# Query ratio on GpSimd, kv products from PSUM column 8, and half of wv issued from ScalarE's queue

## The chip, the cores and the metric

The kernel runs on one core of one Trainium2 chip. The metric is device microseconds of one execution. The kernel before takes 271.44 us (median of 3 runs, 271.33 to 271.71).

## The reference

The input x is 2048 tokens of 640 bf16 numbers. It goes through a layer norm, and then through a linear attention with a learned feature map and through a gated MLP, and the two results are added to x.

```python
xn = layernorm(x)
# A: 32 heads of 20 columns
q, k, v = split(xn @ wqkv)
pq, pk = q @ w_phi, k @ w_phi                      # per head, 20 x 20
phi_q = concat(softmax(pq), softmax(-pq))          # 40 features
phi_k = concat(softmax(pk), softmax(-pk))
kv = phi_k^T @ v ;  z = sum_s phi_k                # per head: 40 x 20 and 40
o = (phi_q @ kv) / (phi_q @ z + 1e-6)
# B
h = silu(xn @ w1) * (xn @ w3)                      # 1536 columns
out = x + o @ wo + h @ w2
```

## The kernel before

**Tiling.** Tokens are cut into 16 tiles `t` of 128 (partitions). The 640 columns are 5 chunks of 128 (`DC`), the 1536 hidden columns 12 chunks (`FC`), and the MLP works on 4 blocks of 512 tokens (`NB`). xn is kept transposed (`xnT`), so that token tiles serve as weights of TensorE and blocks of 512 tokens as moving data. For the kv sums and the query products the 32 heads are taken three at a time, in 11 groups (`NG`, the last has two heads); a head has 20 columns and one for the denominator, so a group has 63 columns, the last 42.

**Stages.** (1) `first_loads` issues the loads: token tile 0 in two halves (one from SyncE's queue, one from ScalarE's), tiles 1 and 2, the two halves of `wv` (the v columns of wqkv), tile 3, the first third of w1 and w3, and so on. Warm-up matmuls on a tile of zeros run meanwhile (`idle`). Tile 0 is normalised on VectorE; the sums of tile 1 are made on ScalarE (`act_sum`). The first four tiles are transposed on TensorE, each followed by its v product in ten matmuls (`v_part`: five with the first half of `wv`, five with the second). (2) `fold_mm` multiplies w_phi into the k and q weights (`Wkp`, `Wqp`). (3) `k_tile` makes the key features, `k_norm` normalises them: VectorE sums (`S`) and takes reciprocals (`rS`), and GpSimd multiplies the features `ekt` with them, two operations for each token tile. (4) `kv_sum` makes kv of all tiles in four parts of four tiles, `kv_store` masks and stores it as `KVc`. (5) For each tile, `q_proj` makes the query features `eq` (ScalarE exponentials), `q_norms` scales them, a transposing DMA makes `eqT`, `q_tok` multiplies them with `KVc` and divides by the denominator, and another transposing DMA makes `oT`. (6) `mlp(b, fc)` is one chunk of the hidden columns of one block: ten matmuls of 512 columns into a pair of PSUM banks, a tanh on ScalarE (`th`), and two VectorE operations (`t1`, in the profile `t`, then `hT`), the first of which reads the first bank of the pair. (7) `out_tile` adds the two output products and x.

**The query scaling.** The two softmaxes differ by a factor for each head only, and one of the two sums cancels against the denominator. So `q_ratio(t)` makes the two sums of a head (`Sq`) by a VectorE reduction, takes the reciprocal of the second on VectorE (`rq`) and multiplies it with the first; `q_scale(t)` then multiplies half of the features with the ratio on GpSimd. Where GpSimd is expected to be free, it adds the two halves of the features before the reduction (`q_half`, tile `half`).

**Order.** No order is written out by hand. Fourteen streams (generators, lines 732 to 916) offer their next step; a planner estimates with costs for each operation when each step could start, takes the earliest, and so lays down one order for each engine. Engines then run their lists in order, with semaphore waits where data or PSUM banks pass from one engine to another. A change of a cost or of an engine can therefore move other steps too. PSUM's 8 banks of 512 f32 columns are used in four pairs; `held` keeps the pair in which kv is summed. The MLP is the stream that fills the time in which TensorE would wait for others.

The operations of the profile are all recorded at line 102 (DMA issues at line 114), so they are told apart by the names of tiles and not by lines.

Of the kernel before, what the change touches and what calls it, by code (L numbers as in the profile page):

```python
# [3 lines left out]
ACT = mybir.ActivationFunctionType  # L4
ALU = mybir.AluOpType
# [4 lines left out]
D = 640  # L10
H = 32
# [6 lines left out]
NG = 11  # L18
# [231 lines left out]
def bass_parallel_sum__linear_kernel_hedgehog__glu_gated_swiglu__prompt_kernel(  # L250
# [16 lines left out]
    P = _Program(nc)  # L267
# [12 lines left out]
    def new(name, shape, dtype, offset=None):  # L280
        size = mybir.dt.size(dtype)
        for n in shape[1:]:
            size *= n
        return P.sbuf(name, shape, dtype, region(size) if offset is None else offset)
# [28 lines left out]
    wv = new("wv", [128, DC, D], bf, RKV + 6400)  # L313
# [10 lines left out]
    eqT = [new(f"eqT{i}", [128, NG, 128], bf, (RKV, RE + 27648)[i // 2] + 5632 + 2816 * (i % 2)) for i in range(4)]  # L324
# [8 lines left out]
    KVc = new("KVc", [128, H * 21], bf, RW)  # L333
# [6 lines left out]
    PS = nc.alloc_psum_tensor("PS", [128, 8 * 512], f32)  # L340
# [3 lines left out]
    def bank(k, cols=512, off=0, rows=128):  # L344
        return PS[0:rows, k * 512 + off:k * 512 + off + cols]
# [5 lines left out]
    def mm(o, l, r, start, stop, shared=False, cost=None):  # L351
        n = free(r)
        P.op("PE", "matmul", [o], [l, r], (o, l, r),
             dict(start=start, stop=stop, skip_group_check=shared),
             cost=max(n / 2400 + 0.003, 0.055) if cost is None else cost)
# [5 lines left out]
    def free(ap):  # L361
        n = 1
        for s in ap.shape[1:]:
            n *= s
        return n
# [5 lines left out]
    def tt(eng, o, a, b, f, fast=1):  # L371
        c = 0.16 + free(o) / 960 / fast if eng == "DVE" else 0.2 + free(o) * 1.7 / 1000
        P.op(eng, "tensor_tensor", [o], [a, b], (o, a, b, f), cost=c)

    def stt(o, a, s, b, f0, f1):
        P.op("DVE", "scalar_tensor_tensor", [o], [a, b], (),
             dict(out=o, in0=a, scalar=s, in1=b, op0=f0, op1=f1), cost=0.16 + free(o) / 960)
# [24 lines left out]
    wqkv_t = A_wqkv.rearrange("(c p) n -> p c n", p=128)  # L402
# [4 lines left out]
    def w13(a, b):  # L407
        P.dma("SP", w1_s[:, :, a:b], w1_t[:, :, a:b])
        P.dma("SP", w3_s[:, :, a:b], w3_t[:, :, a:b])

    def load_x(a, b):
        P.dma("SP", x_tok[:, a:b, :], x_t[:, a:b, :])

    def first_loads():
        def half_wv(a):
            P.dma("SP", wv[:, :, a:a + 320], wqkv_t[:, :, 2 * D + a:2 * D + a + 320])

        P.dma("SP", x_tok[:, 0, 0:320], x_t[:, 0, 0:320])
        P.dma("ACT", x_tok[:, 0, 320:D], x_t[:, 0, 320:D])
        load_x(1, 2)  # L420
        load_x(2, 3)
        half_wv(0)
        half_wv(320)
        load_x(3, 4)
        w13(0, 512)
        P.dma("SP", phi_s[:], phi_t)
        P.dma("SP", wqkT[:, DC:2 * DC, :], A_wqkv[:, D:2 * D], True)
        load_x(4, 8)
        load_x(8, 12)
        load_x(12, 16)  # L430
        P.dma("SP", wqkT[:, 0:DC, :], A_wqkv[:, 0:D], True)
# [152 lines left out]
    def group(g):  # L584
        return 3 * g, min(3, H - 3 * g)
# [46 lines left out]
    def q_sums(t):  # L632
        s = Sq[:, t % 4, :]
        i = eq[t % 4][:].rearrange("p (g c) -> p g c", c=128)[:, :, 0:120].rearrange("p g (n f) -> p g n f", f=DH)
        h = half[:, t % 2, :].rearrange("p (g n f) -> p g n f", n=6, f=10)
        return s[:, 0:66].rearrange("p (g n) -> p g n", n=6), i, h
# [5 lines left out]
    def q_ratio(t, halved):  # L642
        o, i, h = q_sums(t)
        i = h if halved else i
        P.op("DVE", "tensor_reduce", [o], [i], (o, i, AX.X, ALU.add), cost=0.12 + free(i) / 960)
        s = Sq[:, t % 4, :]
        r = rq[:, t % 3, :]
        sv = s[:, 0:64].rearrange("p (h s) -> p h s", s=2)
        P.op("DVE", "reciprocal", [r], [sv[:, :, 1]], (r, sv[:, :, 1]), cost=0.36)
        tt("DVE", r, r, sv[:, :, 0], ALU.mult)  # L650

    def q_scale(t):
        r = rq[:, t % 3, :]
# [10 lines left out]
    def q_tok(t, k):  # L664
        for g in range(NG):
            h, nh = group(g)
            c = 21 * h
            for a, b in ((c, min(c + 21 * nh, 512)), (max(c, 512), c + 21 * nh)):
                if a < b:
                    mm(bank(k, b - a, a), eqT[t % 4][:, g, :], KVc[:, a:b], a in (0, 512), b in (512, 21 * H), True,  # L670
                       max(0.026, (b - a) / 2400 + 0.003))
        p = PS[:, k * 512:k * 512 + 21 * H].rearrange("p (h c) -> p h c", c=21)
        den = den_s[:, t % 2, :]
        sv = Sq[:, t % 4, 0:64].rearrange("p (h s) -> p h s", s=2)
        stt(den, sv[:, :, 0], DEN_EPS, p[:, :, DH], ALU.mult, ALU.add)
        P.op("DVE", "reciprocal", [den], [den], (den, den), cost=0.36)
        tt("DVE", o_tok[:, t % 3, :].rearrange("p (h c) -> p h c", c=DH), p[:, :, 0:DH],
           den.unsqueeze(2).to_broadcast([128, H, DH]), ALU.mult)
# [52 lines left out]

    def norms():
        yield lambda: (first_loads(), consts())
        yield lambda: act_sum(1, ACT.Copy, bst[:, 1, 0:1])
        yield lambda: (ln_half(0, 0), ln_half(0, 1), ln_rstd(0, 1))
# [135 lines left out]
    def q_norms():  # L871
        for t in range(T):
            while done["qp"] <= t:
                yield None
            halved = P.free["POOL"] < P.free["PE"] + 2.0
            if halved:
                yield lambda t=t: q_half(t)
            yield lambda t=t, halved=halved: q_ratio(t, halved)
            yield lambda t=t: q_scale(t)
            done["qn"] = t + 1  # L880
# [8 lines left out]
    def q_toks():  # L889
        for t in range(T):  # L890
            while done["qd"] <= t or not done["kv"]:
                yield None
            yield lambda t=t: q_tok(t, banks(2))
            done["q"] = t + 1
# [129 lines left out]
```

## Time and profile before

| | |
|---|---|
| median of 3 runs | 271.44 us (271.33 to 271.71) |
| the profiled execution | 271.57 us |
| its span, first instruction to last | 269.8 us, 4835 instructions |
| busy: TensorE, VectorE, ScalarE, GpSimd | 263.6, 177.9, 99.6, 97.5 us |
| granted TensorE clock | 1.0 throughout |
| DMA | 27.73 MB, mean 103 GB/s |

In the rows, PE is TensorE (PEld its weight loads), DVE VectorE, ACT ScalarE, POOL GpSimd, SP SyncE; a q behind the name stands for the engine's queue of issues. Times are microseconds from the start of the span. A row of the timeline has start, duration, engine, line, operation, output<-inputs, shapes and count; in brackets stands the idle time of that engine ahead of it and what ended it. Some matmul records are missing (1958 matmuls are shown beside 1978 weight loads): a group of ten may be shown as nine.

### The profile page before, as it was taken

The page shows a single profiled execution, that of the slowest core. Times are in us where ns is not written, and L with a number is a line of the kernel's source. Part 1 is how long each engine was busy: PE and PEld are TensorE (multiplying, and loading weights), DVE is VectorE, ACT ScalarE, POOL GpSimd, SP SyncE. Part 2 cuts the span into 40 slices and gives each one's busy share as a digit, 9 for nine tenths or more (in the row PEclk, how much of TensorE's full clock was granted, in tenths as well). Part 3 has the DMA queues.
Part 4 walks back from the last instruction along what each step waited for, and adds up shares of the span by engine and source line. Part 5 has one row for each costly group of instructions (what it writes and reads, how often), then busy time and mean ns, then how long its engine had stood idle before and what let it go on. Part 6 is the DMA issues. An engine that isn't in the chain of part 4 may idle for free.

```text
span 269.8 us, 4835 instructions
## 1 busy us (share of the span) xinstructions
PE 263.6 (98%) x1958; PEld 161.9 (60%) x1978; DVE 177.9 (66%) x308; ACT 99.6 (37%) x193; POOL 97.5 (36%) x126
## 2 busy tenths in 40 slices
PE   7999999999989999999999999999999999999996
PEld 4656677776736555555555455544577777777774
DVE  4549899998899898888988878878712121212112
ACT  5547979988323434435242434242100000000000
POOL 4225848999993443644444434222000000000000
PEclk9999999999999999999999999999999999999999
DMA  6998695900093255455444460424211313131301
GB/s 193 282 309 179 147 220 116 308 10 2 4 327 72 49 102 80 80 99 102 87 80 89 91 80 10 93 57 78 49 51 52 97 49 97 51 97 49 93 31 49
DMA packets 63510, 27.73 MB, mean 103 GB/s; under 512 B 49792, under 2 KB 63488, under 8 KB 63488
## 3 DMA queue, kind: packets, MB, share of 16 engines
q1 hardware_dynamic: 63344, 27.35, 43.1%
q8 instruction: 15, 0.25, 0.4%
q10 hardware_dynamic: 144, 0.08, 0.1%
q14 instruction: 7, 0.06, 0.1%
HBM read 12.81 MB, written 2.62 MB: 57 GB/s over the span
## 4 chain that ended last, share of the span: by engine, by line
PE 74%; POOL 12%; DVE 9%; issue 3%; DMA 1%; DVEq 0%
PE PS L102 74%; POOL ekt L102 10%; DVE bst L102 4%; DVE x_tok L102 1%; POOL rstd L102 1%; DVE S L102 1%; DMA x_tok<-in_A_x_dram 1%; POOL v L102 1%; DVE hT L102 1%; DVE t L102 1%; DVE Sq L102 1%; DVE mv L102 0%; DVE rS L102 0%; POOL M L102 0%; DVE xres L102 0%
## 5 line engine op out<-in xcount | busy, mean ns | idle before, releaser
L102 PE MATMUL PS<-xnT,w_s 128*128 128x512 bf16 x463 | 105.8, 379 | 1.9 <-DVE t L102 0.8
L102 PEld LDWEIGHTS PS<-xnT,w_s 128*128 128x128 bf16 x480 | 45.5, 98 | 52.2 <-DVE t L102 1.3
L102 PE MATMUL PS<-w_s,hT 128*128 128x320 bf16 (+2 forms) x384 | 54.9, 299 | 0.0
L102 DVE TENSOR_TENSOR xres<-PS,xres 128x640 bf16<-128x640 f32 (+2 forms) x17 | 13.3, 785 | 60.0 <-PE PS L102 60.0
L102 ACT ACTIVATE th<-PS 128x512 f32<-128x512 f32 x48 | 28.8, 600 | 52.4 <-PE PS L102 52.4
L102 PEld LDWEIGHTS PS<-w_s,hT 128*128 128x128 bf16 x384 | 37.6, 98 | 14.6
L102 DVE SCALAR_TENSOR_TENSOR t<-th,PS 128x512 bf16<-128x512 f32 x48 | 32.7, 681 | 15.0 <-ACT th L102 14.6
L102 POOL TENSOR_TENSOR eq<-eq,rq 128x600 bf16<-128x600 bf16 (+1 forms) x32 | 22.6, 727 | 53.8 <-DVE rq L102 53.7
L102 POOL TENSOR_TENSOR ekt<-ekt,rS 128x640 bf16<-128x640 bf16 x32 | 39.5, 1265 | 0.6 <-DVE rS L102 0.6
L102 ACT ACTIVATE eq<-PS 128x600 bf16<-128x600 f32 (+1 forms) x72 | 24.6, 411 | 27.8 <-PE PS L102 27.6
L102 DVE SCALAR_TENSOR_TENSOR hT<-t,PS 128x512 bf16<-128x512 bf16 x48 | 33.0, 687 | 1.8 <-DVE t L102 0.2
L102 PE MATMUL PS<-wv,xnT 128*128 128x320 bf16 x160 | 24.8, 299 | 0.1
L102 PE MATMUL PS<-wo_s,oT 128*128 128x320 bf16 (+2 forms) x160 | 24.5, 299 | 0.0
L102 PE MATMUL PS<-Wkp,xnT 128*128 128x320 bf16 x160 | 23.9, 299 | 0.0
L102 ACT ACTIVATE ekt<-PS 128x640 bf16<-128x640 f32 x32 | 22.3, 703 | 3.8 <-PE PS L102 3.3
L102 PE MATMUL PS<-Wqp,xnT 128*128 128x128 bf16 (+1 forms) x157 | 23.3, 297 | 0.2
L102 DVE TENSOR_REDUCE S<-ekt 128x64 f32<-128x1280 bf16 x16 | 23.0, 1438 | 0.0
L102 POOL TENSOR_TENSOR half<-eq 128x660 f32<-128x660 bf16 x14 | 19.0, 1356 | 8.6 <-ACT eq L102 8.6
L102 PEld LDWEIGHTS PS<-wo_s,oT 128*128 128x128 bf16 x160 | 15.7, 98 | 6.3
L102 PEld LDWEIGHTS PS<-Wqp,xnT 128*128 128x128 bf16 x160 | 12.9, 98 | 10.7
L102 PEld LDWEIGHTS PS<-wv,xnT 128*128 128x128 bf16 x160 | 15.2, 98 | 6.8 <-DVE xnT L102 0.4
L102 PEld LDWEIGHTS PS<-Wkp,xnT 128*128 128x128 bf16 x160 | 15.5, 98 | 6.0
(55 smaller groups left out, 176.9 us busy)
## 6 DMA issues: line engine op xcount, KB each, us to landing
w_s<-in_B_w_dram SPq DMA_DIRECT2D x6, 640.0 KB, 6.2
xres<-in_A_x_dram SPq DMA_DIRECT2D x16, 160.0 KB, 2.3
out_dram<-xres SPq DMA_DIRECT2D x15, 160.0 KB, 1.8
x_tok<-in_A_x_dram SPq DMA_DIRECT2D x3, 640.0 KB, 6.3
w_s<-in_B_w_dram SPq DMA_DIRECT2D x1, 1920.0 KB, 8.0
wv<-in_A_wqkv_dram SPq DMA_DIRECT2D x2, 400.0 KB, 5.4
wo_s<-in_A_wo_dram SPq DMA_DIRECT2D x1, 800.0 KB, 8.4
x_tok<-in_A_x_dram SPq DMA_DIRECT2D x3, 160.0 KB, 3.3
```

The costliest lines, as they stand in the source:

```text
L102: o = _Op(eng, lambda: m(*args, **kw), r, w, cost)
```

## The change

It has three parts.

1. In `first_loads` the first half of `wv` is issued from ScalarE's queue, directly behind ScalarE's half of token tile 0, where it was issued from SyncE's queue behind token tile 2. What follows it on SyncE's queue (the second half of `wv`, tile 3, w1, w3 and all later loads) is issued one place earlier.
2. In `q_ratio` the product of the reciprocal with the first sum is made on GpSimd, where it was on VectorE.
3. In `q_tok` the products lie in PSUM from column 8 of the pair of banks, where they began at column 0. Eight groups of 63 columns are 504, so the border between the banks at column 512 falls between the eighth and the ninth group. Before, it cut the ninth group, which was done in two matmuls of 8 and 55 columns with the same weights. The planner's costs of these matmuls change with it.

```diff
     def first_loads():
-        def half_wv(a):
-            P.dma("SP", wv[:, :, a:a + 320], wqkv_t[:, :, 2 * D + a:2 * D + a + 320])
+        def half_wv(eng, a):
+            P.dma(eng, wv[:, :, a:a + 320], wqkv_t[:, :, 2 * D + a:2 * D + a + 320])
 
         P.dma("SP", x_tok[:, 0, 0:320], x_t[:, 0, 0:320])
         P.dma("ACT", x_tok[:, 0, 320:D], x_t[:, 0, 320:D])
         load_x(1, 2)
         load_x(2, 3)
-        half_wv(0)
-        half_wv(320)
+        half_wv("ACT", 0)
+        half_wv("SP", 320)
         load_x(3, 4)
...
         P.op("DVE", "reciprocal", [r], [sv[:, :, 1]], (r, sv[:, :, 1]), cost=0.36)
-        tt("DVE", r, r, sv[:, :, 0], ALU.mult)
+        tt("POOL", r, r, sv[:, :, 0], ALU.mult)
...
     def q_tok(t, k):
         for g in range(NG):
             h, nh = group(g)
-            c = 21 * h
-            for a, b in ((c, min(c + 21 * nh, 512)), (max(c, 512), c + 21 * nh)):
-                if a < b:
-                    mm(bank(k, b - a, a), eqT[t % 4][:, g, :], KVc[:, a:b], a in (0, 512), b in (512, 21 * H), True,
-                       max(0.026, (b - a) / 2400 + 0.003))
-        p = PS[:, k * 512:k * 512 + 21 * H].rearrange("p (h c) -> p h c", c=21)
+            a, b = 21 * h, 21 * (h + nh)
+            mm(bank(k, b - a, 8 + a), eqT[t % 4][:, g, :], KVc[:, a:b], g in (0, 8), g in (7, NG - 1), True, 0.031)
+        p = PS[:, k * 512 + 8:k * 512 + 8 + 21 * H].rearrange("p (h c) -> p h c", c=21)
```

With the change the planner lays down another order from the query stage on. TensorE's order is the same up to `q_proj(2)`; then an MLP chunk comes ahead of `q_proj(3)` and not behind it, two chunks and not one stand between the products of query tiles 0 and 1, and three and not two follow the last query tile's. On VectorE the reduction of query tile 1 moves behind `kv_store` and is made from GpSimd's `half`, as for the later tiles. On SyncE's queue some transposes `oT` and `eqT` change places.

## The prediction

> **What bounds the kernel now.** The page first: it says which engine fills the span.
>
> ```profile
> span 269.8 us, 4835 instructions
> PE 263.6 (98%) x1958; PEld 161.9 (60%) x1978; DVE 177.9 (66%) x308; ACT 99.6 (37%) x193; POOL 97.5 (36%) x126
> ```
>
> TensorE is busy for 263.6 of 269.8 us. So time can go in two ways only: TensorE gets less to do, or one of its few waits goes. The other engines matter where they make it wait. Next I read the waits of TensorE. The longest one in the middle of the kernel is "PE PS <- DVE t"; the timeline around it shows where it is from.
>
> ```profile
> 62.85 17.22 POOL L102 TENSOR_TENSOR ekt<-ekt,rS 128x640 bf16<-128x640 bf16 x14
> 69.22 4.24 PE L102 MATMUL PS<-v,ekt 128*128 128x63 bf16 x132
> 70.82 0.63 DVE L102 SCALAR_TENSOR_TENSOR t<-th,PS 128x512 bf16<-128x512 f32 x1
> 73.51 6.42 PE L102 MATMUL PS<-xnT,w_s 128*128 128x512 bf16 x29
> 74.57 0.60 ACT L102 ACTIVATE th<-PS 128x512 f32<-128x512 f32 x1 [4.90 <-PE PS L102]
> 75.96 4.16 DVE L102 TENSOR_TENSOR rq<-rq,Sq 128x32 f32<-128x32 f32 x1
> 80.04 0.68 DVE L102 SCALAR_TENSOR_TENSOR t<-th,PS 128x512 bf16<-128x512 f32 x1
> 80.20 1.41 POOL L102 TENSOR_TENSOR eq<-eq,rq 128x600 bf16<-128x600 bf16 x2
> 80.78 2.33 PE L102 MATMUL PS<-xnT,w_s 128*128 128x512 bf16 x10 [0.84 <-DVE t L102]
> 81.64 1.27 SPq L114 DMA_TRANSPOSE eqT<-eq  x1
> 82.94 1.52 PE L102 MATMUL PS<-v,ekt 128*128 128x63 bf16 x44
> ...
> L102 DVE TENSOR_TENSOR rq<-rq,Sq x16: 191/192/4160, 76.0 to 181.9; 128x32 f32<-128x32 f32 x16
> ...
>   DVE rq L102: 53.7, 15
> ```
>
> At 75.96 VectorE begins the product of the ratio of query tile 0. The tile view (min/median/max in ns) says that this operation takes 192 ns, but this one takes 4160: it ends when GpSimd's run of back-to-back key multiplications ends (62.85 + 17.22 = 80.07). Behind it in VectorE's queue stands the first operation on the MLP chunk whose tanh was ready at 75.17. It frees a bank that the fourth chunk needs, so it is late (80.04), and TensorE stops. The thirty matmuls from 73.51 go at 0.216 each (ten from 80.78 to 82.94), so they are issued by 79.99 and the wait is 80.78 - 79.99 = 0.79 us (the row's 0.84 is against the end of the last matmul shown; one record is missing).
>
> The Trainium skill ("SBUF — State Buffer", section "SBUF: two separate sides") says that a VectorE operation with two SBUF inputs and a GpSimd operation that reads SBUF exclude each other for a whole instruction. By that rule alone the wait here would be one GpSimd instruction at most, an estimate of 1.2 us (17.22 / 14), and TensorE would not notice; the row shows 3.97 us beyond the usual 0.19, so here the measured length decides.
>
> **The change, part by part. The ratio on GpSimd.** The operation leaves VectorE. There the tanh's reader, which also runs while GpSimd multiplies (70.82: 0.63 us, no delay), follows the reciprocal at about 75.96 and frees the bank at 76.6, and the fourth MLP chunk needs it at 79.99. The wait of 0.79 us goes; 3.3 us of slack stand in its place. What is late next there is kv's last part: it needs the last key tile (80.07) and is reached at 79.99 + 2.16 = 82.15, so it doesn't wait either. **Term 1: -0.79 us.**
>
> The operation costs GpSimd something that no row shows. The nearest row is a product of 40 columns with the ratio, the farthest plausible one VectorE's own 0.19:
>
> ```profile
> L102 POOL TENSOR_TENSOR eq<-eq,rq 128x40 bf16<-128x40 bf16 x16 | 4.0, 252 | 0.0
> ...
> DMA to landing us min/median/max: 3.5/3.6/5.3
> ...
> 89.18 0.52 PE L102 MATMUL PS<-KVc,eqT 128*128 128x63 bf16 x12
> 89.54 2.32 PE L102 MATMUL PS<-xnT,w_s 128*128 128x512 bf16 x9
> ```
>
> I take 0.25. The sixteen are 4 us, and half of tile 1's features adds one more operation; GpSimd waited 53.7 us for the ratio (the row "DVE rq", above), so the room is there. The wait itself is not new: GpSimd waited for VectorE's product at this place and now waits for VectorE's reciprocal. Behind it in GpSimd's queue stand the scaling and the next tile's `half`; behind the scaling come SyncE's transpose to `eqT` and TensorE's product. For tile 0 the scaling starts 0.25 later (80.45), the transpose is issued at 81.9, and lands 3.6 later (the median of `eqT`) at 85.5. TensorE reaches this product later: kv ends at 82.15 + 44 x 0.031 = 83.5, then ten query-projection steps, ten MLP matmuls and ten more projection steps (1.36 + 2.16 + 1.36) bring it to 88.4. Slack 2.9 us, so I cost it at nothing. If it were uncovered it would cost at most the 0.06 to 0.1 us by which 0.25 exceeds 0.19 plus a hand-over, for each tile: 1.6 us for sixteen.
>
> **The products from column 8.** A tile's products are 11 matmuls and not 12. The 12 take 0.36 us (89.18 to 89.54). For 11, ten of 63 and one of 42 columns, the kv sums are the row: 132 matmuls from 69.22 in 4.24 us, of which the last one's pass is about 0.18, so (4.24 - 0.18) / 131 = 0.031 each and 0.341 for 11. That saves 0.019 a tile. Bounds: nothing, if the pace is set by columns, which stay 672; and a full matmul of 0.031, 0.49 us for sixteen. I take the measured difference, 16 x 0.019. All lie on TensorE's path. **Term 2: -0.30 us.** The VectorE readers keep their shapes.
>
> **Half of wv from ScalarE's queue.** Here are the rows of the first 10 us, and one further on for the pace; below them stand the landing times of wv and three stretches of the windows view (length; busy us and count of PE, PEld, DVE, ACT, POOL; granted clock; DMA share; GB/s).
>
> ```profile
> 0.79 1.35 SPq L114 DMA_DIRECT2D x_tok<-in_A_x_dram  x3
> 0.79 0.39 ACTq L114 DMA_DIRECT2D x_tok<-in_A_x_dram  x1
> 1.21 1.28 ACT L102 ACT_TABLE_LOAD   x1 [1.21 <-PEq L1009]
> 2.19 1.00 SPq L114 DMA_DIRECT2D wv<-in_A_wqkv_dram  x2
> 3.65 0.74 ACT L102 ACTIVATE t<-x_tok 128x640 bf16<-128x640 bf16 x1 [0.93 <-DMA x_tok<-in_A_x_dram]
> 4.52 0.14 DVE L102 TENSOR_SCALAR mv<-bst 128x1 f32<-128x1 f32 x1
> 5.30 0.45 DVE L102 TENSOR_SCALAR x_tok<-x_tok,mv,rstd 128x640 bf16<-128x640 bf16 x1 [0.63 <-POOL rstd L102]
> 5.88 0.56 POOL L102 TENSOR_TENSOR rstd<-rstd,mhalf 128x1 f32<-128x1 f32 x1 [0.62 <-DVE rstd L102]
> 6.30 0.94 PE L102 MATMUL PS<-t 128*128 128x128 bf16 x8
> 6.76 0.44 DVE L102 TENSOR_SCALAR x_tok<-x_tok,mv,rstd 128x640 bf16<-128x640 bf16 x1
> 7.30 0.13 PEld L102 LDWEIGHTS PS<-wv,xnT 128*128 128x128 bf16 x2 [0.24 <-issue]
> 7.33 0.43 PE L102 MATMUL PS<-wv,xnT 128*128 128x320 bf16 x2
> 7.60 0.44 PE L102 MATMUL PS<-ident,x_tok 128*128 128x128 bf16 x5
> 8.43 1.06 PEld L102 LDWEIGHTS PS<-wv,xnT 128*128 128x128 bf16 x9 [0.32 <-DMA wv<-in_A_wqkv_dram]
> 8.85 0.49 DVE L102 BATCH_NORM_STATS2 bst<-x_tok 128x6 f32<-128x320 bf16 x1 [0.83 <-DMA x_tok<-in_A_x_dram]
> 9.75 0.28 PEld L102 LDWEIGHTS PS<-ident,x_tok 128*128 128x128 bf16 x5 [0.25 <-DVE x_tok L102]
> 22.57 1.66 PE L102 MATMUL PS<-Wkp,xnT 128*128 128x320 bf16 x11
> ...
> DMA to landing us min/median/max: 5.0/5.4/5.7
> ...
> 4.00:4.50 0.50, 0.50 (x4) 0.30 (x3) 0.43 (x3) 0.47 (x2) 0.00 (x0) 1.00 0.74 172
> 4.50:5.00 0.50, 0.50 (x8) 0.50 (x6) 0.16 (x2) 0.30 (x1) 0.31 (x1) 1.00 0.94 291
> ...
> 30.00:40.00 10.00, 10.00 (x75) 7.15 (x74) 9.55 (x20) 8.55 (x13) 5.36 (x11) 1.00 0.95 202
> ```
>
> The two halves of wv are issued at 2.19 and about 2.67 and land (5.0 and 5.7 later) at 7.2 and 8.4. Both are waited for. TensorE's eight fillers from 6.30 end at 7.24, and a matmul can follow while the last one drains, at about 7.13 (estimate: 0.94 / 8 ahead of that end); it goes at 7.33, just behind the first landing: 0.20 us. The second half is waited for at 8.43; and tile 3, next in the queue, lands at 8.83, VectorE's statistics at 8.85 wait for it, the normalisation of tile 2 stands behind them, and the transposes at 9.75 wait for that. From 7.33 to 9.75 TensorE issues 14 matmuls of 320 columns, at (1.66 - 0.30) / 10 = 0.136 each by the row at 22.57, and five transposes, some 0.28 by the row at 7.60 less its last pass. That is 2.18 of 2.42 us: 0.24 lost. So at most 0.44 us can be had.
>
> How much comes depends on the DMA engines. Between 3.5 and 4.5 us they are not full (172 GB/s at 4.00 against 291 in the next half microsecond, DMA share 0.74): about (291 - 172) x 0.5 = 60 KB to make good there and about as much in the half before, which at 291 is 0.4 us. With the first half issued at about 1.2 from ScalarE and everything behind it on SyncE about 0.47 earlier, that hole can be filled, and the second half and tile 3 land by up to 0.4 earlier. Against that stand tiles 1 and 2, whose transfers now run beside wv's. Tile 1 landed just ahead of 3.65. If it comes later by d, ScalarE's sums, VectorE's operation at 4.52 (0.64 us of room ahead of 5.30) and the rest follow; the factor of tile 1 is ready at 6.44 and used at 6.76 (0.32 of room), and the transposes at 7.60 follow its end at 7.20 with 0.3 more. So d under 0.6 costs nothing. ScalarE's second issue, like the first, takes some 0.4 us; the table load then ends at 2.9 and the small activation behind it still lies within the 0.93 us that ScalarE waited for tile 1.
>
> Bounds of this part: -0.44, and +0.4 if tile 1 waits behind the whole half of wv (d = 1.2, the distance of the two landings of wv): tile 0's normalisation is then 0.56 late, tile 1's transposes start at about 8.1, and the second half of v(0) at 8.8 and not 8.43. I take nearer the first end, because tile 1, the second of SyncE's three issues from 0.79, goes out at about 1.25, before ScalarE would be done issuing (about 1.6): **Term 3: -0.25 us.** All loads and all steps on VectorE and GpSimd behind it move along, and where TensorE is full, as from 30 to 40 us (10.00 of 10.00), a shift of its whole queue is kept.
>
> The Trainium skill ("DMA: Bandwidth & Descriptors", section "Issuing engines are not separate DMA queues") speaks against this part: transfers from different issuing engines run on the same 16 DMA engines and interleave, and a second issuing engine saves only the time of issuing. By that rule the term is between 0 and the loss above; it is the first rival.
>
> **Sum.** -0.79 - 0.30 - 0.25 = -1.34 us against the profiled execution of 271.57 us (span 269.8 and 1.8 around it, which stays): 270.23. The profiled execution is 0.13 above the median of the runs, 271.44, so on that scale I say **270.1 us**.
>
> **Rivals.**
> 1. *The start gains nothing or loses*: wv's half shares the DMA engines with tiles 1 and 2, and what TensorE no longer waits for wv it waits for tile 1. For it: both are wanted within 4 us and the DMA share is 0.94 at 4.5. Against it: the hole at 4.00. Time: -1.09 with +0 to +0.4, that is 270.35 to 270.75. Chance 0.25.
> 2. *The stall only changes its victim*: what holds VectorE from 75.96 to 80.12 is not this operation, and the next one, the tanh's reader, is held instead. Against it: that operation ran in 0.63 us at 70.82 in the same GpSimd run, and fifteen ratio products, at times without that run, take 0.19. Terms 2 and 3 remain: 270.9. Chance 0.05.
> 3. *Slower*: the query chain becomes the bound. Reciprocal, GpSimd's product, scaling, transpose and product lie in a row, and in the new order the products of some tiles could come up before their `eqT` has landed. It decides from where the slack of a tile is used up; to end above 272.0 (slower by 0.2%) it must eat the 1.34 and 0.54 more, 1.9 us or 0.12 for every tile. For it: the new chain is longer by 0.06 to 0.1 and `eqT` takes up to 5.3. Against: the view of `eqT` shows no wait of TensorE for it now, and for tile 0 I found 2.9 of slack. With 0.13 a tile, 2.1 us, the time is 272.2. Chance 0.05.
> 4. *The same without slowing*: the same chain, with only a few tiles late, 0.3 to 0.9 us in all: 270.4 to 271.0. Chance 0.1.
>
> **How the numbers follow.** My forecast has 0.55. The likeliest time is 270.1. Low: all gains at their ends, -0.79 - 0.49 - 0.44 = -1.72, gives 269.7. High: term 2 at nothing and the start at +0.4 gives 271.44 - 0.39 = 271.05. The range 269.7 to 271.1 leaves out rival 3 and little else. About 0.2% (0.54 us) is what a measurement here can tell from no change: faster means below 270.9. Forecast, rival 1 (nearly all), most of rival 4 and half of rival 2 lie there: 0.85. Same 0.1, slower 0.05.
>
> **What would show it.** The profile after should show no wait of TensorE between 79 and 81 us, the chunk behind the first tanh read at about 76, sixteen ratio products on GpSimd of 0.2 to 0.3 us, 176 and not 192 products with KVc, and in the first 10 us the weight loads for wv at about 7.1 and 8.1. Wrong would be: a VectorE operation of several us in the same place, weight loads with KVc that wait for a DMA, or tile 1's sums later than 4.2 and the first v matmul not earlier than 7.33.

## The result and the profile after

The changed kernel takes 269.67 us (median of 6 runs, 269.60 to 269.82) beside 271.40 us before (6 runs, 271.21 to 271.71): ratio 0.9936, 95% interval 0.9923 to 0.9949, or 1.74 us less (1.38 to 2.09). Measured again on another occasion the ratio was 0.9947 (0.9935 to 0.9959). The prediction was 270.1 us with a range of 269.7 to 271.1: the direction is right, and the time lies just below the range. The ratio and the products gain clearly; the gain of the start is small, and the runs alone do not tell it from nothing.

The page of the kernel after, its first lines and the chain that ended last; below them the same chain in the kernel before:

```profile
span 268.0 us, 4821 instructions
PE 263.9 (98%) x1962; PEld 161.2 (60%) x1962; DVE 171.0 (64%) x292; ACT 99.5 (37%) x193; POOL 102.9 (38%) x143
PE 96%; DMA 1%; ACT 1%; DVE 0%; POOL 0%; issue 0%; SPq 0%
...
PE 74%; POOL 12%; DVE 9%; issue 3%; DMA 1%; DVEq 0%
```

VectorE is busy for 6.9 us less (177.9 to 171.0), 4.2 of which were the one long operation, and GpSimd for 5.4 us more; TensorE's busy time is the same within what missing records allow. The chain is now TensorE nearly all the way, 96% where it was 74%.

The timeline around the wait of before, in the kernel after:

```profile
68.76 4.24 PE L102 MATMUL PS<-v,ekt 128*128 128x63 bf16 x132
72.82 8.32 PEld L102 LDWEIGHTS PS<-xnT,w_s 128*128 128x128 bf16 x40
72.84 8.79 PE L102 MATMUL PS<-xnT,w_s 128*128 128x512 bf16 x40
75.12 0.35 DVE L102 RECIPROCAL rq<-Sq 128x32 f32<-128x32 f32 x1
75.39 0.63 DVE L102 SCALAR_TENSOR_TENSOR t<-th,PS 128x512 bf16<-128x512 f32 x1
79.59 0.24 POOL L102 TENSOR_TENSOR rq<-rq,Sq 128x32 f32<-128x32 f32 x1
79.92 1.41 POOL L102 TENSOR_TENSOR eq<-eq,rq 128x600 bf16<-128x600 bf16 x2
81.47 1.51 PE L102 MATMUL PS<-v,ekt 128*128 128x63 bf16 x44
87.71 0.50 PE L102 MATMUL PS<-KVc,eqT 128*128 128x63 bf16 x11
88.05 2.32 PE L102 MATMUL PS<-xnT,w_s 128*128 128x512 bf16 x10
...
L102 POOL TENSOR_TENSOR rq<-rq,Sq x16: 242/252/256, 79.6 to 178.0; 128x32 f32<-128x32 f32 x16
```

The tanh's reader follows the reciprocal (75.39), forty MLP matmuls run as one block of 8.79 us, and the ratio products take 0.25 us each on GpSimd. From the first kv sums to the last part of them it is 81.47 - 68.76 = 12.71 us; before it was 82.94 - 69.22 = 13.72.

That is 1.01 us and not the predicted 0.79. The row that settles it belongs to the profile before. It shows the weight loads of the thirty matmuls that stand ahead of the wait:

```profile
73.27 6.17 PEld L102 LDWEIGHTS PS<-xnT,w_s 128*128 128x128 bf16 x30
```

Thirty loads are shown, from 73.27, beside 29 matmuls from 73.51. The missing matmul is the first one. So the thirty are issued from about 73.30 and done by 73.30 + 30 x 0.216 = 79.78, and the wait is 80.78 - 79.78 = 1.00 us. The profile with column 8 alone, further down, has the same wait and all thirty matmuls, from 73.11: 80.60 - (73.11 + 30 x 0.216) = 1.01 us.

The first 10 us after, the pace row further on, and the landing times of wv's first half, its second half and tile 1, in this order:

```profile
1.22 0.46 ACTq L114 DMA_DIRECT2D wv<-in_A_wqkv_dram  x1
4.01 0.74 ACT L102 ACTIVATE t<-x_tok 128x640 bf16<-128x640 bf16 x1 [0.80 <-DMA x_tok<-in_A_x_dram]
6.66 0.45 PE L102 MATMUL PS<-wv,xnT 128*128 128x320 bf16 x2
7.35 0.45 PE L102 MATMUL PS<-ident,x_tok 128*128 128x128 bf16 x5 [0.25 <-DVE x_tok L102]
7.64 1.79 PE L102 MATMUL PS<-wv,xnT 128*128 128x320 bf16 x12
9.29 0.28 PEld L102 LDWEIGHTS PS<-ident,x_tok 128*128 128x128 bf16 x5 [0.19 <-DVE x_tok L102]
22.12 1.11 PE L102 MATMUL PS<-Wkp,xnT 128*128 128x320 bf16 x7
...
DMA to landing us min/median/max: 4.4/4.4/4.4
DMA to landing us min/median/max: 5.5/5.5/5.5
DMA to landing us min/median/max: 2.8/2.8/2.8
```

The first half of wv lands at 5.6 (7.2 before), the second at 7.7 (8.4), tile 1 at 4.0 (3.6). TensorE waits for wv no more; it waits 0.25 us for tile 1's normalisation instead. The first Wkp matmul is at 22.12, 0.45 us earlier than in the profile before.

### The profile page after: what moved, and what is told of

It is laid out like the page before. It is cut to its first block, busy times and chain, and to the rows that moved or that the text cites. A ratio compares the mean times of both kernels' runs of the same rounds, so it can differ in the third digit from the quotient of the medians.

```text
span 268.0 us, 4821 instructions
## 1 busy us (share of the span) xinstructions
PE 263.9 (98%) x1962; PEld 161.2 (60%) x1962; DVE 171.0 (64%) x292; ACT 99.5 (37%) x193; POOL 102.9 (38%) x143
## 4 chain that ended last, share of the span: by engine, by line
PE 96%; DMA 1%; ACT 1%; DVE 0%; POOL 0%; issue 0%; SPq 0%
PE PS L102 96%; DMA x_tok<-in_A_x_dram 1%; ACT t L102 1%; POOL rstd L102 0%; DVE x_tok L102 0%; DVE xres L102 0%; SPq L114 0%; DVE rstd L102 0%; DVE mv L102 0%
## 5 line engine op out<-in xcount | busy, mean ns | idle before, releaser
L102 PE MATMUL PS<-xnT,w_s 128*128 128x512 bf16 x480 | 107.5, 379 | 0.0
L102 PE MATMUL PS<-Wqp,xnT 128*128 128x512 bf16 (+1 forms) x160 | 24.1, 299 | 0.0
L102 POOL TENSOR_TENSOR rq<-rq,Sq 128x32 f32<-128x32 f32 x16 | 4.0, 252 | 48.8 <-DVE rq L102 48.8
L102 POOL TENSOR_TENSOR half<-eq 128x660 f32<-128x660 bf16 x15 | 20.4, 1358 | 3.6 <-ACT eq L102 3.6
```

Source lines behind the costliest of these rows:

```text
L102: o = _Op(eng, lambda: m(*args, **kw), r, w, cost)
```

## Experiments

### The ratio on GpSimd alone

```diff
-        tt("DVE", r, r, sv[:, :, 0], ALU.mult)
+        tt("POOL", r, r, sv[:, :, 0], ALU.mult)
```

> The kernel before with the ratio product on GpSimd for all 16 query tiles; wv and the product columns as before. Theory: what this part brings is the wait of TensorE at 80 us, read again with the profile after as 1.0 us (80.78 less 73.30 plus thirty matmuls of 0.216; the missing record stood ahead of 73.51, not behind it), so 270.4 us, with VectorE's first chunk operation at about 76.0 and the matmuls of the MLP from 73.3 to 82 us without a gap. Rival, only the victim changes: the operation behind the reciprocal is held until about 80.1 instead, and the time is within 0.2 of before. Rival, it works only along with the other two parts (another order): under half of 1.0.

Measured: 270.12 us beside 271.22, ratio 0.9957 (0.9944 to 0.9971), that is 1.17 us less (0.79 to 1.52). The MLP matmuls in its timeline:

```profile
72.82 8.79 PE L102 MATMUL PS<-xnT,w_s 128*128 128x512 bf16 x40
75.39 0.63 DVE L102 SCALAR_TENSOR_TENSOR t<-th,PS 128x512 bf16<-128x512 f32 x1
81.45 1.51 PE L102 MATMUL PS<-v,ekt 128*128 128x63 bf16 x44
```

One block of forty; no other operation became the victim. The theory holds, with 1.0 us for this part.

### The ratio on GpSimd for query tile 0 alone

```diff
-        tt("DVE", r, r, sv[:, :, 0], ALU.mult)
+        tt("POOL" if t == 0 else "DVE", r, r, sv[:, :, 0], ALU.mult)
```

> The kernel before with the ratio product on GpSimd for query tile 0 alone; the other fifteen stay on VectorE. Theory (the gain is one held operation): the same as with all sixteen on GpSimd, 270.4 us, within 0.2. Rival (the gain comes from the 7 us that VectorE has less to do, spread over the query stage): about a sixteenth of it, 271.3 us.

Measured: 270.21 us, ratio 0.9964 (0.9951 to 0.9976), 0.98 us less (0.65 to 1.33). Moving one operation of the sixteen brings what all sixteen bring, within the intervals. The other fifteen, 0.19 us each or 2.9 us less for VectorE, are worth nothing that these runs show.

```profile
73.20 8.79 PE L102 MATMUL PS<-xnT,w_s 128*128 128x512 bf16 x40
```

### The products from column 8 alone

The diff is that of `q_tok` in the change.

> The kernel before with the products from PSUM column 8 alone. Theory: 16 tiles times 0.0226 us (12 matmuls in 0.364, 11 in 0.342 start to start), 0.36 us less: 271.05 us; the wait at 80 us stays. Rival of the prediction, 0.30: 271.1 us, which this run can hardly tell from it; rival, columns set the pace: 271.4 us. Rival, the new order of the query stage by itself moves something: more than 0.2 away from 271.05.

Measured: 270.80 us, ratio 0.9984 (0.9975 to 0.9992), 0.43 us less (0.22 to 0.68). The runs do not tell 0.36 from 0.30. The profiles do: from a tile's first product to the next matmul it was 89.54 - 89.18 = 0.36 before and is 88.05 - 87.71 = 0.34 after; summed start to start over the sixteen tiles, and with the missing records of before put at 0.216 each, 5.83 and 5.47 us, so 0.36 less. The wait stays where it was:

```profile
73.11 6.63 PE L102 MATMUL PS<-xnT,w_s 128*128 128x512 bf16 x30
75.78 4.17 DVE L102 TENSOR_TENSOR rq<-rq,Sq 128x32 f32<-128x32 f32 x1
80.60 2.33 PE L102 MATMUL PS<-xnT,w_s 128*128 128x512 bf16 x10 [0.85 <-DVE t L102]
```

### Half of wv from ScalarE alone

The diff is that of `first_loads` in the change.

> The kernel before with the first half of wv issued from ScalarE alone; every engine's order of computing stays the same. Theory: the whole start moves by 0.45 us as in the profile after (first Wkp matmul at 22.12 and not 22.57) and nothing behind it takes it back: 270.95 us. Rival, the prediction's 0.25: 271.15 us. Rival, the shift is lost at the wait of 80 us, because what ends it, GpSimd's run, does not move along: 271.4 us.

Measured: 271.09 us, ratio 0.9993 (0.9985 to 1.0002), 0.19 us less (from 0.41 less to 0.05 more). Its own profile starts Wkp at 21.92, 0.65 us ahead of the profile before, which shows that one pair of profiles says little here: the landing times differ from one execution to the next.

```profile
21.92 1.25 PE L102 MATMUL PS<-Wkp,xnT 128*128 128x320 bf16 x8
75.32 4.16 DVE L102 TENSOR_TENSOR rq<-rq,Sq 128x32 f32<-128x32 f32 x1
80.13 2.33 PE L102 MATMUL PS<-xnT,w_s 128*128 128x512 bf16 x10 [0.86 <-DVE t L102]
```

The early start is kept: GpSimd's run ends earlier too, and the wait is as long as before. The rival that it is lost there falls.

### The change once more, and without the wv part

```diff
-        half_wv("ACT", 0)
+        half_wv("SP", 0)
```

> The changed kernel once more, to stand on the same chip beside the two variants of its first loads. All theories: its ratio to the kernel before within the interval of the first measurement, 0.9923 to 0.9949. Its profile adds one more look at the landing times: the theory of the start says tile 1 lands later than 3.7 us, the second half of wv ahead of 7.8 and tile 3 ahead of 8.2.

> The changed kernel with both halves of wv on SyncE's queue again (ratio on GpSimd and column 8 stay). Theory (the start term is a few tenths, as the runs of that part alone had it: 0.19 us, -0.05 to 0.41): slower than the changed kernel by 0.2 to 0.4 us, first Wkp matmul at 22.1 to 22.6. Rival (the start term is what the single pair of profiles showed): 0.45 slower. Rival (nothing, the transfers only interleave): the same within 0.1.

Measured: the changed kernel 269.75 us, ratio 0.9947 (0.9935 to 0.9959); without the wv part 270.04 us, ratio 0.9960 (0.9946 to 0.9974). The difference is 0.29 us, with intervals that overlap. With the runs of this part alone and the start in the profiles it can be narrowed. The moments in us, each from one profiled execution:

| | wv from SyncE: before, and the runs with ratio, ratio of tile 0, column 8, no wv part | wv from ScalarE: after, after again, wv alone, and the two probes below |
|---|---|---|
| tile 1 lands | 3.62, 3.59, 3.57, 3.54, 3.57 | 3.99, 3.88, 3.78, 3.90, 3.97 |
| second half of wv lands | 8.39, 7.87, 8.28, 8.19, 8.05 | 7.66, 7.42, 7.46, 7.60, 7.35 |
| tile 3 lands | 8.83, 8.32, 8.73, 8.64, 8.51 | 8.12, 7.87, 7.93, 8.06, 7.81 |
| first Wkp matmul | 22.57, 22.10, 22.48, 22.39, 22.25 | 22.12, 22.08, 21.92, 22.03, 22.11 |

The means of the last line are 22.36 and 22.05: 0.31 us. The profile before happened to be the latest of its five. The second half of wv and tile 3 land 0.65 us earlier, tile 1 lands 0.33 later, and the five of one side overlap with those of the other only in the last line, by a few hundredths.

The same profiles can be cut at the first Wkp matmul, at the first matmul of kv's last part and at the end of the span. The lengths in us:

| | to Wkp | Wkp to kv's last part | from there to the end |
|---|---|---|---|
| before | 22.57 | 60.37 | 186.89 |
| ratio alone | 22.10 | 59.35 | 186.89 |
| ratio of tile 0 alone | 22.48 | 59.35 | 186.89 |
| column 8 alone | 22.39 | 60.38 | 186.53 |
| wv alone | 21.92 | 60.38 | 186.89 |
| without the wv part | 22.25 | 59.35 | 186.52 |
| after | 22.12 | 59.35 | 186.53 |
| after again | 22.08 | 59.35 | 186.52 |

So the ratio brings 1.02 us and the products 0.36, each in its own stretch and whatever the other parts are. What differs beyond that between these profiles lies ahead of Wkp. There the earlier first half of wv brings nothing that can be seen: the weight loads of tile 1's transposes start at 7.25 us in the mean of the five profiles with wv from SyncE and at 7.27 in the five with wv from ScalarE. Those of tile 2's start at 9.53 and 9.21. The 0.3 us come from the second half and tile 3, which land earlier.

### Tile 1 from ScalarE as well

```diff
-        load_x(1, 2)
+        P.dma("ACT", x_tok[:, 1:2, :], x_t[:, 1:2, :])
         load_x(2, 3)
```

> The changed kernel with token tile 1 also issued from ScalarE's queue, between its half of tile 0 and the half of wv. Theory (wv's half, sharing the DMA engines, delays tile 1, and tile 1's transposes are what TensorE waits for at 6.9 us): tile 1 no longer competes and lands at about 3.6, the gap ahead of its transposes shrinks from 0.41 us to under 0.2, and the kernel is 0.1 to 0.3 us faster than the changed one. Rival (behind that wait stands another, tile 2's normalisation, which follows tile 3's statistics): no change, within 0.1. Rival (three issues ahead of the table load make ScalarE late for tile 1's sums): slower by 0.1 to 0.3.

Measured: 270.77 us beside 269.75 of the changed kernel, ratio to before 0.9995 (0.9977 to 1.0013): slower by a microsecond, and neither for the theory's reason nor for a rival's. Nine of its twelve runs took 270.3 to 271.1 us and three 272.4 to 272.6; the profiled one took 272.60, so its rows show more than the loss of the median. In it tile 1 lands later, at 4.5, and the first half of wv not at all early:

```profile
8.48 0.69 PE L102 MATMUL PS<-wv,xnT 128*128 128x320 bf16 x2 [1.59 <-DMA wv<-in_A_wqkv_dram]
8.97 0.74 PE L102 MATMUL PS<-ident,x_tok 128*128 128x128 bf16 x5
24.96 0.71 PE L102 MATMUL PS<-Wkp,xnT 128*128 128x320 bf16 x4
...
9.00:10.00 1.00, 1.00 (x8) 0.80 (x7) 0.74 (x3) 0.26 (x1) 0.31 (x1) 0.50 1.10 347
...
L114 ACTq DMA_DIRECT2D wv<-in_A_wqkv_dram x1: 456/456/456, 1.7 to 1.7; - x1
...
DMA to landing us min/median/max: 6.6/6.6/6.6
DMA to landing us min/median/max: 6.1/6.1/6.1
```

Both halves of wv are now issued at 1.7, one from each queue, and land at 8.3 and 7.8; in the changed kernel they land at 5.6 and 7.7. Issued together, both land about when the later one does in the changed kernel, or later still. The Trainium skill ("DMA: Bandwidth & Descriptors", section "Issuing engines are not separate DMA queues") says that transfers issued by different engines run on the same 16 DMA engines and interleave; the trace agrees. In the changed kernel the half that is needed first is issued about a microsecond ahead of the other (1.22 and 2.17). In this profile TensorE then waits 1.59 us, and its next matmuls run at half their pace (0.107 and not 0.056 for a transpose; 0.74 and not 0.44 for the five), at a granted clock of 0.50. The two stretches behind Wkp are 59.35 and 186.53, as in the changed kernel, so all that this execution loses, it loses ahead of Wkp. What the nine shorter runs lose, no profile shows.

### Probes: what holds VectorE

The changed kernel, with one more operation on VectorE behind the reciprocal of key tile 12; nobody reads its result.

```diff
+        if t == 12:
+            tt("DVE", s[:, 0:32], s[:, 0:32], r[:, 0:32], ALU.mult)
```

> The changed kernel with one probe on VectorE: behind the reciprocal of key tile 12, in the middle of GpSimd's back-to-back key multiplications, a product of the same size as the ratio (128x32 f32) with both inputs in SBUF, whose result nobody reads. GpSimd has about three tiles, 7 us, of work in its queue there. Theory (such an operation does not get in between back-to-back GpSimd operations and waits until GpSimd's queue runs dry): the probe takes 5 to 7 us. Rival (it is excluded for one whole GpSimd operation): 1.5 us at most. Rival (what held the ratio product was something of that place, the end of the key stage): 0.19 us.

```diff
+        if t == 12:
+            P.op("DVE", "tensor_scalar", [s[:, 0:32]], [r[:, 0:32]], (),
+                 dict(out=s[:, 0:32], in0=r[:, 0:32], scalar1=EPS, scalar2=None, op0=ALU.add), cost=0.19)
```

> The same probe place as with two inputs (behind the reciprocal of key tile 12, GpSimd back to back), but the operation has one input in SBUF (reciprocals plus a constant, 128x32 f32). Theory (two SBUF inputs are what makes it wait): 0.1 to 0.2 us, like the reciprocals and reductions around it. Rival (any VectorE operation that writes f32 to SBUF with two operands or in a fast mode is held): several us, as the one with two inputs.

Timelines of the kernel with two inputs, then with one (there the fourth matmul stands in two rows, and the last line is one microsecond of the windows view):

```profile
57.43 14.78 POOL L102 TENSOR_TENSOR ekt<-ekt,rS 128x640 bf16<-128x640 bf16 x12
64.94 0.55 DVE L102 RECIPROCAL rS<-S 128x64 f32<-128x64 f32 x1 [0.56 <-POOL ekt L102]
65.53 6.73 DVE L102 TENSOR_TENSOR S<-S,rS 128x32 f32<-128x32 f32 x1
74.32 4.95 POOL L102 TENSOR_TENSOR ekt<-ekt,rS 128x640 bf16<-128x640 bf16 x4 [2.11 <-DVE rS L102]
81.80 2.33 PE L102 MATMUL PS<-xnT,w_s 128*128 128x512 bf16 x10 [2.41 <-DVE t L102]
```

```profile
57.51 14.78 POOL L102 TENSOR_TENSOR ekt<-ekt,rS 128x640 bf16<-128x640 bf16 x12
65.61 6.72 DVE L102 TENSOR_SCALAR S<-rS 128x32 f32<-128x32 f32 x1
81.86 1.21 PE L102 MATMUL PS<-xnT,w_s 128*128 128x512 bf16 x4 [2.39 <-DVE t L102]
82.52 3.11 PE L102 MATMUL PS<-xnT,w_s 128*128 128x512 bf16 x7
...
83.00:84.00 1.00, 1.00 (x4) 0.31 (x3) 0.96 (x3) 0.47 (x1) 1.00 (x3) 0.50 0.00 0
```

Both probes end when GpSimd's run ends (57.43 + 14.78 = 72.21 and 65.53 + 6.73 = 72.26): they get in only when GpSimd's queue has run dry, which it does because the next reciprocals stand behind the probe. So it is not the place (the rival of 0.19 falls) and not one GpSimd operation's length (1.5 us falls). That only two inputs make an operation wait falls as well: one input and a constant wait just as long. What sets the held operations apart from those that pass stays open. Reciprocals, reductions and the tanh's reader, which takes one of its inputs from PSUM, pass in the same run. The two kernels took 272.2 and 273.9 us, each in one execution. From Wkp to the end that is 2.6 and 4.2 us more than in the changed kernel; 1.6 us of the second is TensorE's slower clock behind the wait.

## Why the prediction was wrong

- **Term 1, the wait at 80 us: right in kind, mis-sized.** The operation, its cause and its disappearance are as predicted, and the slack of kv's last part holds (81.47, GpSimd's run over at 79.6). The step that failed is "they are issued by 79.99 and the wait is 80.78 - 79.99 = 0.79 us": it counts thirty matmuls from 73.51, and the missing record was the first of the thirty, ahead of 73.51. The wait was 1.0 us and not 0.79. The step "low: all gains at their ends" failed with it, for it gave this term no end beyond 0.79. With 1.0 there the low end would have been 269.5 and held the 269.67.
- **Term 2, the products: mis-sized by little.** 0.36 and not 0.30: 0.019 a tile was the difference of 0.36 and 0.341 with one digit too few; it is 0.0226. The bounds held it.
- **Term 3, the start: the size right, with luck.** Predicted 0.25 between +0.4 and -0.44; the runs give 0.19 (wv alone) and 0.29 (taken out of the changed kernel), neither clear of zero, and the profiles 0.31. Tile 1 lands later by 0.33, within the d under 0.6 that was to cost nothing, and ScalarE has the room that was given. But that lateness did cost: it took what the first half of wv was to bring (0.20), since tile 1's transposes start no earlier. The whole gain is the other wait, for the second half and tile 3, put at 0.24. Their landings moved by 0.65, more than the 0.4 given; the chain of tile 1 and then of tile 2 on VectorE took the rest, since the transposes at 7.35 and 9.29 now wait for it.
- **Sum.** 1.02 + 0.36 + 0.31 is 1.69, within both measured intervals; 271.40 less 1.69 is 269.71, just inside the range; the 0.04 us to the measured 269.67 are less than these runs can tell. The three parts alone gave 1.17, 0.43 and 0.19, 1.79 in all, so they neither help nor hinder each other as far as the runs tell.
- **Rivals.** 1 (the start gains nothing): true of the first half of wv; for the whole start the profiles speak against it, though the runs of wv alone cannot exclude zero. 2 (another victim): excluded by the ratio alone. 3 and 4 (the query chain): TensorE has no wait for `eqT`; the stage from the last kv sums on is shorter by term 2 alone (186.89 and 186.53 us).

## What to carry to other kernels

Look through the view of a tile for an operation whose longest time is twenty times its median: such a one may be waiting inside itself, as here, where no row of waits named it, and moving it alone brought what moving all sixteen did. When a matmul record is missing, count the weight loads of the same stretch before a wait is sized, and give that term a bound too. A load that is moved to a second queue lets those behind it land earlier and those beside it later, so look at both: here the later tile 1 took what the earlier first half of wv could bring. When a span varies from one execution to the next, cut it at fixed moments: the stretches that do not vary show a gain to a hundredth of a microsecond.

## What the runs showed of the hardware

- VectorE operations on 128x32 f32 stood for 4.16, 6.73 and 6.72 us beside back-to-back GpSimd multiplications of 1.27 us each, until GpSimd's queue was empty; the first of them, the ratio product, takes 0.19 us elsewhere. In a back-to-back run VectorE did not get its turn in between: the waits are 3 to 5 of GpSimd's instructions.
- The Trainium skill ("SBUF — State Buffer", section "SBUF: two separate sides") names which VectorE operations and GpSimd instructions exclude each other for a whole instruction: those with two SBUF inputs, against one that reads SBUF, or in a two-port fast mode. The two held products have two SBUF inputs and fit that; in which mode the held operation with one input ran, no run shows. The length does not fit: where the skill speaks of one whole instruction, the waits here were three to five of them.
- After a wait of 2.39 us (the probe with one input) TensorE ran three matmuls of 512 columns at its full pace of about 0.22 us, one in 0.345 and the next six at 0.427, with a granted clock of 0.50 from 83 to 86 us. After a wait of 2.41 us (the probe with two) all ten ran at about 0.216. From the first of the ten to the first of the query projection behind kv's last part it is 5.18 us and 3.53: the same wait cost 1.6 us more in one execution than in the other.
